# First feed-forward product as seven block products over two row blocks, with row sums shared with the keys, and the second product as a phase of its own fed from DRAM

## The chip, the cores and the metric

The kernel runs on one core of one Trainium2 chip. The metric is the device time of one execution in microseconds; three executions of the kernel before took 507.57, 507.62 and 509.29 us, and the median, 507.62 us, is the number to compare with. TensorE (PE) multiplies matrices, VectorE (DVE), ScalarE (ACT) and GpSimd (POOL) work on tiles of up to 128 partitions, and SyncE (SP) issues nearly all transfers between DRAM and the on-chip memories: SBUF, and PSUM, into which TensorE accumulates.

## The reference

A row x (2048 rows of 512) goes through two branches that a gate mixes:

```python
q, k, v = split(x @ wqkv)                        # 32 heads of 16
phi(t) = [softmax(t @ w_phi), softmax(-t @ w_phi)]
a = (phi(q) @ (phi(k).T @ v)) / (phi(q) @ sum(phi(k)) + 1e-6) @ wo
r = relu(x @ w1 + b1); b = (r * r) @ w2 + b2     # 512 -> 1792 -> 512
g = sigmoid((x * gate_w).sum(-1)); out = g * a + (1 - g) * b
```

All of it is float32. Each operand of a large product is split into two float32r tiles, hi (a copy that ACT makes) and lo (source minus hi, one subtraction), and `mm3` issues three matmuls, hi·hi, hi·lo and lo·hi, into one PSUM tile.

## The kernel before

The rows stand in four blocks of 512 (b), each of four chunks of 128 (c). Blocks of 128 of the 1792 hidden columns are numbered fc (14 of them). The kernel makes two sweeps over the row blocks, sweep 0 with fc 0 to 6 and sweep 1 with fc 7 to 13. In each step of a sweep `up` multiplies one fc of w1 with one row block: four k-slices of 128 by three matmuls of 128x512, so 12 matmuls into one PSUM tile u. `hidden` (L457) turns u into the second product's input: ACT adds the bias and takes relu, squares, and copies hi; DVE subtracts lo (L464). `down` then multiplies that pair with w2 for the four chunks, 12 more matmuls, two steps after (LAG). Sweep 0's results go to a DRAM tile `part` and come back in sweep 1.

Between these steps stand the pieces of the attention branch. In sweep 0 keys and values of two chunks at a time (a pair) come from seven block products of a Strassen-Winograd scheme, p1 to p7, instead of eight: `product` (L549) multiplies row blocks A11, A12, A22 or sums S1 to S4 of them with weight blocks B or differences T1 to T4. The sums of rows are made on POOL (`rows_make`, L276), those of weights on DVE (`sums_make`, L257), before their splits. `features` computes phi(k) on DVE and ACT, `do_kv` accumulates phi(k).T v. In sweep 1 `do_q` and `q_phi` make phi(q) (with two POOL multiplications per chunk, L387), `numer` and `attended` the output of the branch.

The order of all this is written out: `at(slot, f, ...)` puts a piece at a half step of the sweeps, and `tc.issue_after` and `tc.high_priority` bind single instructions; the framework's scheduler orders the rest and sets the waits. Each engine works its own queue strictly in order, so an instruction that waits holds all behind it, on SP too. The weights w1, w2 are split once; lo is kept in DRAM (`lkept`) and hi is copied again from the reloaded source.

Of the kernel before, what the change touches and what calls it, by code (L numbers as in the profile page):

```python
# [23 lines left out]
NFH = NF // 2  # L24
LAG = 2
NG = 8
VW = DH + 1
NV = 2
NPAIR = S // P // 2
NSTR = 3  # L30
AHEAD = 150
FOLD_AT = 9, 3
KEPT_LATE = ("w1", 0), ("w1", 1), ("w2", 0)
SUMS = ("t1", "t2", "t15", "k2")
# [3 lines left out]
def tile_gated_mix(ctx: ExitStack, tc: tile.TileContext, xT, xn, wqT, wkT, wphi, wv, wo, w1, b1, w2, b2, gw, out):  # L38
# [3 lines left out]
    stage = pool("stage", 4)  # L42
    xpool = pool("xpool", 2 * NK)
    wpool = pool("wpool", 1)
    fpool = pool("fpool", NSTR)
# [3 lines left out]
    ps_d = pool("ps_d", NC, space=PSUM)  # L49
    ps_u = pool("ps_u", 2, space=PSUM)  # L50
    ps_a = pool("ps_a", 1, space=PSUM)
    ps_b = pool("ps_b", 1, space=PSUM)
    banks = [ps_a, ps_b]
    st, up_w, down_w = {}, {}, {}
    taken = [0]

    def bank(name):
        p = banks[taken[0] % len(banks)]
        taken[0] += 1
        return p.tile([P, 512], F32, tag="s", name=name)  # L60

    def split(src, hi, lo, ehi, elo):
        if ehi is nc.scalar:
            i = nc.scalar.activation(hi, src, AF.Copy)
        else:
            i = ehi.tensor_copy(hi, src)
        st["low"] = elo.tensor_tensor(lo, src, hi.bitcast(F32), ALU.subtract)  # L70
        return i

    def mm3(o, a, b, sa, sb, first, last, **kw):
        (ah, al), (bh, bl) = a, b
        nc.tensor.matmul(o, ah[:, sa], bh[:, sb], start=first, stop=False, **kw)  # L75
        nc.tensor.matmul(o, ah[:, sa], bl[:, sb], start=False, stop=False, **kw)  # L76
        return nc.tensor.matmul(o, al[:, sa], bh[:, sb], start=False, stop=last, **kw)  # L77

    ALL = slice(0, 512)
    halves = (slice(0, 256), slice(256, 512))  # L80


    def load(src):
        t = stage.tile([P, 512], F32, tag="in", name="in")
        nc.sync.dma_start(t, src)
        return t

    def row():
        return work.tile([P, D], F32, tag="row", name="row", bufs=6)

    def slots(op, kk, name, dtype=F32R):
        return [wpool.tile([P, 512], dtype, tag=f"{op}{kk}{j}", name=f"{name}{j}") for j in "hl"]

    def ffn_tiles(nm, fc):
        if fc >= NFH + NSTR:
            return slots(("B21", "T1", "T4", "T3")[fc - NFH - NSTR], int(nm == "w2"), f"{nm}{fc}")
        return (fpool.tile([P, 512], F32R, tag=nm + "h", name=f"{nm}h{fc}"),
                fpool.tile([P, 512], F32R, tag=nm + "l", name=f"{nm}l{fc}"))

    raw = {}

    def fetch(nm, fc, t=None):
        src = w1[fc] if nm == "w1" else w2[fc * P:(fc + 1) * P, :]
        if t is None:
            t = load(src)
        else:
            nc.sync.dma_start(t, src)
        raw[nm, fc] = t  # L110

    def keep(nm, fc):
        nc.sync.dma_start(lkept[fc, int(nm == "w2")], (up_w if nm == "w1" else down_w)[fc][1].bitcast(F32))

    def again(nm, fc):
        fetch(nm, fc)
        hi, lo = raw[nm, fc, "hl"] = ffn_tiles(nm, fc)
        nc.sync.dma_start(lo.bitcast(F32), lkept[fc, int(nm == "w2")])

    def again_ready(nm, fc):  # L120
        hi, lo = raw.pop((nm, fc, "hl"))
        with tc.issue_after(st["act"].ins):
            nc.scalar.activation(hi, raw.pop((nm, fc)), AF.Copy)
        (up_w if nm == "w1" else down_w)[fc] = hi, lo

    def ready(nm, fc, elo=nc.vector):
        hi, lo = ffn_tiles(nm, fc)
        i = split(raw.pop((nm, fc)), hi, lo, nc.scalar, elo)
        (up_w if nm == "w1" else down_w)[fc] = hi, lo
        return i  # L130

    def ready_later(nm, fc, *elo):
        with tc.issue_after(st["act"].ins):
            ready(nm, fc, *elo)

    def x_tiles(b, k):
        return (xpool.tile([P, SB], F32R, tag="xh", name=f"xh{b}_{k}"),
                xpool.tile([P, SB], F32R, tag="xl", name=f"xl{b}_{k}"))


    def x_save(b):
        for k in range(NK):
            for j in range(2):
                nc.sync.dma_start(xkept[b, k, j], st["x", b][k][j].bitcast(F32))

    def load_x(b):
        xs = []
        for k in range(NK):
            xs.append(x_tiles(b, k))
            for j in range(2):  # L150
                nc.sync.dma_start(xs[k][j].bitcast(F32), xkept[b, k, j])
        return xs


    def x_fetch(b):
        for k in range(NK):
            if k % 2 == 0:
                t = work.tile([P, 2 * D], F32, tag="tb", name="xin", bufs=2)
                st.setdefault(("xr", b), []).append(t)
            raw["x", b, k] = t[:, (k % 2) * D:(k % 2 + 1) * D]  # L160
            nc.sync.dma_start(raw["x", b, k], xT[b, :, k, :])
# [40 lines left out]
    def fold(nm, groups=range(NK)):  # L202
# [19 lines left out]
        if groups[-1] < NK - 1:  # L222
            return
# [648 lines left out]
```

## Time and profile before

| | us |
|---|---|
| median of three executions | 507.62 |
| profiled execution, first to last instruction (span) | 505.0 |
| PE busy | 500.7 |
| DVE busy | 405.2 |
| ACT busy | 253.9 |
| POOL busy | 75.6 |
| DMA, all queues, share of 16 engines | 52% |

The profiled execution's time is its span; the 2.6 us between it and the median lie ahead of the first and behind the last instruction and are taken as the same for both kernels. In the rows of the profile a line begins with the engine or the time, then the code line, the operation, and tile out<-in; "xh", "w1h" are hi tiles, "xl", "w1l" lo tiles. Durations of neighbouring rows on an engine may overlap by some tens of nanoseconds, so the distance of two starts is what one costs.

### The profile page before, as it was taken

The numbers are of one execution on the slowest core, as the hardware profiler recorded it, in microseconds if no ns is written. First come the engines' busy times: TensorE is split into PE (matmuls) and PEld (weight loads), VectorE is DVE, ScalarE is ACT, GpSimd is POOL, SyncE is SP. The second block draws the span as 40 slices with busy tenths as digits, with TensorE's granted clock in tenths as the row PEclk, the third lists the DMA queues.
The fourth block names the chain that finished last, engine by engine and source line by source line (L and its number), as shares of the span: only waits on it lengthen the run. The fifth ranks groups of instructions, "written<-read, shape, count | busy, mean of one in ns | idle before, by whom it ended". The sixth has DMA issues, their size and how long they took to land.

```text
span 505.0 us, 9519 instructions
## 1 busy us (share of the span) xinstructions
PE 500.7 (99%) x3616; PEld 404.0 (80%) x3616; DVE 405.2 (80%) x642; ACT 253.9 (50%) x433; POOL 75.6 (15%) x77
## 2 busy tenths in 40 slices
PE   9999999999999999999999999999999999999997
PEld 4878887788888888888888878787887878788876
DVE  4979996898877868797889898968789677798724
ACT  6598573364743646373765653443425353433530
POOL 5304020302050000000004122202122222202100
PEclk9999999999999999999999999999999999999999
DMA  8998888965657656845669161212153321032102
GB/s 296 331 361 299 232 283 270 321 234 192 212 183 245 236 165 208 279 140 155 187 183 311 51 195 52 91 51 92 39 185 96 86 74 44 8 100 82 43 22 83
DMA packets 52437, 84.79 MB, mean 168 GB/s; under 512 B 8104, under 2 KB 14504, under 8 KB 52392
## 3 DMA queue, kind: packets, MB, share of 16 engines
q1 hardware_dynamic: 52072, 83.79, 51.5%
q8 instruction: 28, 0.46, 0.4%
q10 hardware_dynamic: 288, 0.39, 0.3%
q14 instruction: 17, 0.14, 0.1%
q0 software_dynamic: 32, 0.01, 0.0%
HBM read 56.37 MB, written 21.50 MB: 154 GB/s over the span
## 4 chain that ended last, share of the span: by engine, by line
PE 97%; ACT 1%; DMA 1%; DVE 0%; issue 0%
PE d L75 10%; PE u L75 10%; PE d L77 10%; PE d L76 10%; PE u L76 10%; PE u L77 10%; PE q L75 3%; PE q L77 3%; PE att L77 3%; PE q L76 3%; PE att L76 3%; PE att L75 3%; PE ky L75 2%; PE ky L76 2%; PE ky L77 2%; PE kvps L378 2%
## 5 line engine op out<-in xcount | busy, mean ns | idle before, releaser
L459 ACT ACTIVATE r<-u,b1c 128x512 f32<-128x512 f32 x56 | 38.4, 685 | 146.1 <-PE u L77 146.0
L387 POOL TENSOR_TENSOR ez<-e,z 128x512 f32<-128x512 f32 x32 | 41.3, 1312 | 279.8 <-ACT e L358 160.5
L75 PE MATMUL d<-w2h,hh 128*128 128x512 f32 x160 | 62.7, 392 | 0.0
L77 PE MATMUL d<-w2h,hl 128*128 128x512 f32 x160 | 62.3, 389 | 0.0
L76 PE MATMUL d<-w2l,hh 128*128 128x512 f32 x160 | 62.3, 389 | 0.0
L75 PE MATMUL u<-xh,w1h 128*128 128x512 f32 x152 | 59.6, 392 | 0.1
L76 PE MATMUL u<-xl,w1h 128*128 128x512 f32 x152 | 59.2, 389 | 0.0
L77 PE MATMUL u<-xh,w1l 128*128 128x512 f32 x152 | 59.2, 389 | 0.0
L363 DVE TENSOR_REDUCE sm<-e 128x64 f32<-128x1024 f32 x32 | 38.9, 1215 | 18.5 <-ACT e L358 18.5
L464 DVE TENSOR_TENSOR hl<-r,hh 128x512 fp32r<-128x512 f32 x56 | 38.5, 687 | 13.8 <-ACT hh L463 13.7
L411 ACT ACTIVATE phiT<-tb 32x256 f32<-32x256 f32 x64 | 26.5, 413 | 32.1 <-DVE tb L405 31.4
L358 ACT ACTIVATE e<-e 128x1024 f32<-128x1024 f32 x32 | 33.8, 1056 | 11.9 <-DVE e L356 11.6
L463 ACT ACTIVATE hh<-r 128x512 fp32r<-128x512 f32 x56 | 35.3, 630 | 1.5
L460 ACT ACTIVATE r<-r 128x512 f32<-128x512 f32 x56 | 35.2, 629 | 1.3
L75 PEld LDWEIGHTS d<-w2h,hh 128*128 128x128 f32 x160 | 30.0, 188 | 6.7 <-issue 0.6
L77 PEld LDWEIGHTS d<-w2h,hl 128*128 128x128 f32 x160 | 30.0, 188 | 6.3
L76 PEld LDWEIGHTS d<-w2l,hh 128*128 128x128 f32 x160 | 30.1, 188 | 6.1
L75 PEld LDWEIGHTS u<-xh,w1h 128*128 128x128 f32 x152 | 28.5, 188 | 7.6 <-issue 0.8
L276 POOL TENSOR_TENSOR row<-xin 128x256 f32<-128x256 f32 x16 | 17.5, 1103 | 112.8 <-DVE S2ol L70 24.8
L77 PEld LDWEIGHTS u<-xh,w1l 128*128 128x128 f32 x152 | 28.5, 188 | 6.1
L76 PEld LDWEIGHTS u<-xl,w1h 128*128 128x128 f32 x152 | 28.5, 188 | 5.8
L389 DVE TENSOR_REDUCE dz<-ez 128x64 f32<-128x1024 f32 x16 | 19.4, 1210 | 9.4 <-POOL ez L387 9.3
(544 smaller groups left out, 1161.6 us busy)
## 6 DMA issues: line engine op xcount, KB each, us to landing
in<-in_w SPq DMA_DIRECT2D x66, 256.0 KB, 3.3
phiT<-tb SPq DMA_DIRECT2D x192, 32.0 KB, 1.9
w2l<-lkept SPq DMA_DIRECT2D x20, 256.0 KB, 3.7
w1l<-lkept SPq DMA_DIRECT2D x19, 256.0 KB, 4.4
xin<-in_xT SPq DMA_DIRECT2D x16, 256.0 KB, 5.0
xkept<-xh SPq DMA_DIRECT2D x16, 256.0 KB, 3.6
xkept<-xl SPq DMA_DIRECT2D x16, 256.0 KB, 4.0
in<-in_xn SPq DMA_DIRECT2D x16, 256.0 KB, 2.8
```

Source lines behind the costliest of these rows:

```text
L75: nc.tensor.matmul(o, ah[:, sa], bh[:, sb], start=first, stop=False, **kw)
L76: nc.tensor.matmul(o, ah[:, sa], bl[:, sb], start=False, stop=False, **kw)
L77: return nc.tensor.matmul(o, al[:, sa], bh[:, sb], start=False, stop=last, **kw)
L358: nc.scalar.activation(ef, ef, AF.Exp)
L363: nc.vector.tensor_reduce(sm, e3, AX.X, ALU.add)
L387: nc.gpsimd.tensor_tensor(ez[:, hs, :], e3[:, hs, :], zbc[half], ALU.mult)
L389: nc.vector.tensor_reduce(dz, ez, AX.X, ALU.add)
L411: nc.scalar.activation(dst, src, AF.Copy)
L459: nc.scalar.activation(r, ps, AF.Relu, bias=b1c[:, fc:fc + 1])
L460: nc.scalar.activation(r, r, AF.Square)
L463: st["act"] = nc.scalar.activation(hh, r, AF.Copy)
L464: low = lambda: st.update(low=nc.vector.tensor_tensor(hl, r, hh.bitcast(F32), ALU.subtract))
```

## The change

The first product is put into the same seven-product scheme as the keys and values. The 512 columns of x are halves 1 and 2, the rows of two row blocks are halves 1 and 2, and two fc make one pair g (7 pairs, 2 row pairs r: 14 units u = (r, g)). A unit is seven products of two k-slices by three matmuls, 42 matmuls, where four cells of `up` were 48. Its x operands A11, A12, A22, S1 to S4 are 512 columns wide and are the same tiles that the keys' products read (128 columns of them at a time). Its weight operands per pair are O0 (B11 and B21), O1 (T1 and B22), O2 (T2 and T3) and O3 (T4), made by `w_sums` and `w_last`, mostly on POOL, split, and written to DRAM (`wkept`, `wkept4`) for the second row pair, which reads them back (`w_again`).

The seven results of a unit are combined by adds: t1 is copied by ACT, t15 and t2 are copied by ACT and added to t1 on POOL (`u_half`, L220), three outputs are added on DVE (`u_out`, L211). `hidden` now only does relu and square, in place, and the float32 result goes to a DRAM tile `hkept` (56 tiles of 256 KB). The weight sums of keys and values (`k_ready`) move to POOL.

There are now three phases: an opening (units (0,0) to (0,2), no key products), a phase where the items of `u_stream` and `v_stream` alternate (units of r = 0, then r = 1, with eight key/value pairs of two chunks), and a phase for the second product, queries and output, where `h_fetch` loads each h tile from DRAM, ACT copies hi and POOL subtracts lo (`h_ready`). `part` and the sweeps are gone. TensorE's queue is the order in which the code is written (`manual_schedule`); the other queues are ordered by the framework.

```diff
+    def w_sums(g, eng, tag=None):
+        a, b = raw["w", g, 0], raw["w", g, 1]
+        t = raw["w", g, 2] = ring("T23in") if tag is None else slot(tag, "T23in")
+        eng.tensor_tensor(t[:, RIGHT], b[:, RIGHT], b[:, LEFT], ALU.subtract)
+        eng.tensor_tensor(b[:, LEFT], b[:, LEFT], a[:, LEFT], ALU.subtract)
+        eng.tensor_tensor(t[:, LEFT], b[:, RIGHT], b[:, LEFT], ALU.subtract)
...
+    def uproduct(ps, g, p, first, last):
+        xo, wop = PAIRS[p]
+        t, at = w_op(g, wop)
+        for kk in range(2):
+            mm3(ps, t, st["X", xo, kk], slice(at + kk * P, at + (kk + 1) * P), ALL, first and kk == 0, last and kk == 1,
+                skip_group_check=True)
...
+    def hidden(t, b, f, src):
+        nc.scalar.activation(t, src, AF.Relu, bias=b1c[:, f:f + 1])
+        nc.scalar.activation(t, t, AF.Square)
+        nc.sync.dma_start(hkept[b, f], t)
...
+    def u_half(u, p, key, bankkey):
+        st[bankkey, u] = ubank("u" + bankkey)
+        uproduct(st[bankkey, u], u[1], p, True, False)
+        t = st[key, u] = work.tile([P, 512], F32, tag="ol", name=key, bufs=2)
+        with ahead():
+            nc.scalar.activation(t, st[bankkey, u], AF.Copy)
+            nc.gpsimd.tensor_tensor(t, t, st["t1", u], ALU.add)
...
-    def sums_make(kk, early):
-        k1, k2, v1, v2 = st["w", "k"][kk], st["w", "k"][2 + kk], raw["v", kk], raw["v", 2 + kk]
-        t1, t4 = [raw.setdefault((op, kk), row()) for op in ("T1", "T4")] if early else (raw["T1", kk], raw["T4", kk])
-        raw["T2", kk], raw["T3", kk] = v2, v1
-        for o, x, y in ((t1, v1, k1), (v1, v2, v1)) if early else ((v2, v2, t1), (t4, k2, v2)):
-            nc.vector.tensor_tensor(o, x, y, ALU.subtract)
+    def k_ready(op, kk, eng):
+        k1, k2, v1, v2 = st["w", "k"][kk], st["w", "k"][2 + kk], raw["v", kk], raw["v", 2 + kk]
+        if op == "T1":
+            eng.tensor_tensor(k1, v1, k1, ALU.subtract)
+        elif op == "T3":
+            eng.tensor_tensor(v1, v2, v1, ALU.subtract)
+        elif op == "T2":
+            eng.tensor_tensor(v2, v2, k1, ALU.subtract)
+        elif op == "T4":
+            eng.tensor_tensor(k2, k2, v2, ALU.subtract)
...
+    def h_ready(t):
+        hi, lo = st["h", t] = [work.tile([P, 512], F32R, tag=f"O{t % 2}{j}", name="h" + j, bufs=2) for j in "hl"]
+        split(raw["h", t], hi, lo, nc.gpsimd)
...
+    UP = ("p1", "p5", "p6", "p4", "p2", "p7", "p3")
+    VP = ("p1", "p6", "p5", "p2", "burst", "p7", "p3", "p4")
```

What stands in the queues is shown at three places of the opening. First POOL. Before, these eight rows (sums of two column pieces of x for the first two pairs of chunks, L276) are all of POOL's arithmetic until four more such rows some 25 us later:

```order
L276 TENSOR_TENSOR row_279<-xin_134,xin_135 128x256
L276 TENSOR_TENSOR row_280<-xin_134 128x256
L276 TENSOR_TENSOR row_279<-row_279,xin_134 128x256
L276 TENSOR_TENSOR row_376<-xin_134,xin_135 128x256
L276 TENSOR_TENSOR row_280<-xin_135,row_279 128x256
L276 TENSOR_TENSOR row_376<-row_376,xin_134 128x256
L276 TENSOR_TENSOR row_377<-xin_134 128x256
L276 TENSOR_TENSOR row_377<-xin_135,row_376 128x256
```

Now the queue holds six 128x512 sums of x (S1, S2, S4), nine 128x256 sums of w1 and four t15/t2 adds, and behind these the twelve rows below, up to T2 (L283) of both k-slices:

```order
L152 TENSOR_TENSOR T23in_621<-w1in_508 128x256
L153 TENSOR_TENSOR w1in_508<-w1in_508,w1in_506 128x256
L154 TENSOR_TENSOR T23in_621<-w1in_508 128x256
L279 TENSOR_TENSOR wkin_464<-wvin_155,wkin_464 128x512
L220 TENSOR_TENSOR t15_535<-t15_535,t1_242 128x512
L281 TENSOR_TENSOR wvin_155<-wvin_156,wvin_155 128x512
L283 TENSOR_TENSOR wvin_156<-wvin_156,wkin_464 128x512
L158 TENSOR_TENSOR w1in_506<-w1in_506,T23in_621 128x256
L220 TENSOR_TENSOR t2_583<-t2_583,t1_242 128x512
L279 TENSOR_TENSOR wkin_464<-wvin_155,wkin_464 128x512
L281 TENSOR_TENSOR wvin_155<-wvin_156,wvin_155 128x512
L283 TENSOR_TENSOR wvin_156<-wvin_156,wkin_464 128x512
```

That is 31 rows (18 of 128x512, 13 of 128x256) where there were eight of 128x256. Second DVE, at the split of the same operand T2. Before, DVE makes the differences itself (L257) and splits right behind them (L70):

```order
L257 TENSOR_TENSOR wvin_224<-wvin_224,row_426 128x512
L257 TENSOR_TENSOR wvin_224<-wvin_224,row_430 128x512
L257 TENSOR_TENSOR row_427<-wkin_353,wvin_224 128x512
L257 TENSOR_TENSOR row_431<-wkin_353,wvin_224 128x512
L70 TENSOR_TENSOR T20l_499<-wvin_224,T20h_498 128x512
L70 TENSOR_TENSOR B210l_503<-wkin_353,B210h_502 128x512
L70 TENSOR_TENSOR T21l_507<-wvin_224,T21h_506 128x512
```

Now the splits (L57) wait for POOL's differences, mixed with the unit outputs c (L211), and T2's second slice is the 52nd row of DVE's queue:

```order
L57 TENSOR_TENSOR O0l_607<-w1in_506,O0h_606 128x512
L57 TENSOR_TENSOR KB111l_515<-wkin_464,KB111h_514 128x512
L57 TENSOR_TENSOR O1l_669<-w1in_508,O1h_668 128x512
L57 TENSOR_TENSOR KT10l_520<-wkin_464,KT10h_519 128x512
L211 TENSOR_TENSOR c_616<-uY_576,t15_535 128x512
L57 TENSOR_TENSOR KT11l_525<-wkin_464,KT11h_524 128x512
L57 TENSOR_TENSOR KT31l_565<-wvin_155,KT31h_564 128x512
L211 TENSOR_TENSOR c_631<-uZ_528,t2_583 128x512
L57 TENSOR_TENSOR KT20l_588<-wvin_156,KT20h_587 128x512
L57 TENSOR_TENSOR KT21l_593<-wvin_156,KT21h_592 128x512
```

Third PE, where the first product with T2 stands (p6 of the first key pair, tile ky before, kY now). Before, it stands inside a cell of the first product (u), after two of its matmuls:

```order
L75 MATMUL u_609<-xh0_0_164,w1h6_534 128x512
L76 MATMUL u_609<-xl0_0_165,w1h6_534 128x512
L75 MATMUL ky_644<-T20h_498,S0oh0_368 128x512
L76 MATMUL ky_644<-T20l_499,S0oh0_368 128x512
L77 MATMUL ky_644<-T20h_498,S0ol0_370 128x512
```

Now it is the 22nd whole product, counted from unit (0,1)'s p1, with p5 of unit (0,3) ahead of it and that unit's p6 (tile uY_722, operand O2) behind:

```order
L61 MATMUL uZ_701<-S11h_231,O1h_668 128x512
L62 MATMUL uZ_701<-S11l_232,O1h_668 128x512
L63 MATMUL uZ_701<-S11h_231,O1l_669 128x512
L61 MATMUL kY_713<-KT20h_587,S20h_264 128x512
L62 MATMUL kY_713<-KT20l_588,S20h_264 128x512
L63 MATMUL kY_713<-KT20h_587,S20l_265 128x512
L61 MATMUL kY_713<-KT21h_592,S21h_268 128x512
L62 MATMUL kY_713<-KT21l_593,S21h_268 128x512
L63 MATMUL kY_713<-KT21h_592,S21l_269 128x512
L61 MATMUL uY_722<-S20h_264,O2h_681 128x512
```

Products of six matmuls have taken the place of cells of twelve, and TensorE's queue can't pass T2's product before both slices of T2 are split.

1174 lines of the change are left out of this document (618 added, 556 removed).

## The prediction

> **What bounds the kernel now.** I read the page first: busy times, the slices, and the chain that ended last.
>
> ```profile
> span 505.0 us, 9519 instructions
> ...
> PE 500.7 (99%) x3616; PEld 404.0 (80%) x3616; DVE 405.2 (80%) x642; ACT 253.9 (50%) x433; POOL 75.6 (15%) x77
> ...
> DVE  4979996898877868797889898968789677798724
> ...
> POOL 5304020302050000000004122202122222202100
> PEclk9999999999999999999999999999999999999999
> ...
> PE 97%; ACT 1%; DMA 1%; DVE 0%; issue 0%
> ```
>
> TensorE is busy all the time at its full granted clock and is 97% of the chain. Busy alone could hide small waits, so next the view of waits for PE, the chain's first and last pieces, and four neighbouring matmuls of the timeline:
>
> ```profile
> PE warm L500 <- PEq L861: 0.8, 1, 0.8
> PE u L527 <- DMA win<-in_w: 0.3, 1, 0.3
> ```
>
> ```profile
> 5.42 3.70 PE u L527 x8
> ...
> 17.34 1.84 PE foldk L211 x102
> ...
> 501.89 0.48 DVE row L817
> ```
>
> ```profile
> 182.81 0.39 PE L75 MATMUL u<-xh,w1h 128*128 128x512 f32 x1
> 183.04 0.39 PE L76 MATMUL u<-xl,w1h 128*128 128x512 f32 x1
> 183.26 0.39 PE L77 MATMUL u<-xh,w1l 128*128 128x512 f32 x1
> 183.49 0.39 PE L75 MATMUL u<-xh,w1h 128*128 128x512 f32 x1
> ```
>
> Three matmuls start within 183.49 - 182.81 = 0.68 us, so one costs 0.2267 us, not its 0.39. From 5.42 to 501.89 the profile names no wait for PE of over a microsecond. **The kernel is bound by the number of matmuls**: every one saved is worth 0.2267 us as long as its operands keep coming in time, and every wait that appears is added in full.
>
> **The change, part by part.**
>
> *Matmuls.* Before, the first product is 14 x 4 cells of 12; now it is 14 units of 42. One whole cell of float32 matmuls at the start (L527) stays, in place of a unit's p1 and p2 and worth 12 in both. So 672 - 588 = 84 matmuls go. Keys, queries, output and the second product keep theirs. 84 x 0.2267 = **-19.0 us**. That is all the change can win.
>
> *The opening.* Here POOL gets work that it didn't have, and DVE's splits run beside it. What they do to each other shows in the timeline of both engines, in three stretches:
>
> ```profile
> 12.55 1.22 DVE L70 TENSOR_TENSOR w2l<-win,w2h 128x512 fp32r<-128x512 f32 x1
> 14.11 0.81 DVE L464 TENSOR_TENSOR hl<-r,hh 128x512 fp32r<-128x512 f32 x1 [0.34 <-ACT hh L463]
> 14.85 1.22 DVE L70 TENSOR_TENSOR w1l<-in,w1h 128x512 fp32r<-128x512 f32 x1
> ...
> 37.71 0.69 DVE L464 TENSOR_TENSOR hl<-r,hh 128x512 fp32r<-128x512 f32 x1
> 38.31 0.69 DVE L70 TENSOR_TENSOR w1l<-in,w1h 128x512 fp32r<-128x512 f32 x1
> ...
> 43.72 0.68 DVE L354 TENSOR_REDUCE mn<-kx 128x32 f32<-128x512 f32 x1
> 44.32 0.68 DVE L355 TENSOR_TENSOR e<-kx,mx 128x512 f32<-128x512 f32 x1
> ```
>
> ```profile
> 13.19 1.19 POOL L276 TENSOR_TENSOR row<-row,xin 128x256 f32<-128x256 f32 x1
> 14.34 1.18 POOL L276 TENSOR_TENSOR row<-xin 128x256 f32<-128x256 f32 x1
> ...
> 43.88 0.74 POOL L276 TENSOR_TENSOR row<-row,xin 128x256 f32<-128x256 f32 x1
> 44.58 0.75 POOL L276 TENSOR_TENSOR row<-xin 128x256 f32<-128x256 f32 x1
> ...
> 270.21 2.54 POOL L387 TENSOR_TENSOR ez<-e,z 128x512 f32<-128x512 f32 x2 [2.42 <-DVE dz L389]
> ```
>
> Alone, a DVE split costs 38.31 - 37.71 = 0.60 us, a POOL sum of 256 columns 44.58 - 43.88 = 0.70, one of 512 columns 2.54 / 2 = 1.27. At 12 to 16 us both engines work on two SBUF tiles at once, and there a split lasts 1.22 and a POOL sum 1.18: POOL starts one each 14.34 - 13.19 = 1.15 us, about a sum and a split one after the other. At 44 us DVE reads PSUM, and neither is slowed. So two-SBUF-tile operations of DVE and POOL take turns. A pair of a 256-column sum and a split costs 1.15 us; with a 512-column sum 1.27 - 0.70 = 0.57 more, 1.72.
>
> The Trainium skill, page "SBUF — State Buffer", section "Who interferes with whom", says the same against this change: a DVE instruction with two SBUF inputs and a GpSimd instruction that reads SBUF exclude each other for the whole instruction. By it the opening is the turn-taking sum below, 45.9 us and not POOL's 32.0 alone. The rows at 12 to 16 us agree.
>
> Up to T2's last split the change's queues hold 31 POOL sums (18 of 512 columns, 13 of 256), and from the first of them on 35 DVE rows with two SBUF tiles (30 of 512). Pairing them: 13 x 1.15 + 18 x 1.72 = 45.9 us. Start:
>
> ```profile
> 7.90 1.88 POOL L276 TENSOR_TENSOR row<-xin 128x256 f32<-128x256 f32 x2 [4.81 <-DMA xin<-in_xT]
> ```
>
> ```profile
> GB/s 0 0 38 197 246 303 398 379 358 355 402 396 393 402 391 393 385 377 339 396 391 396 393 369 290 145 243 363 350 328 257 268 347 385 284 216 238 371 377 322
> ```
>
> Before, POOL starts at 7.90, when the four tiles of the first row block have landed. S1 needs tiles of the second row block, up to the ninth of the opening's 256 KB loads. The view of the DMA over the first 30 us (0.75 us a slice) reaches 9 x 0.262 MB at 9.2 us; I take 9.5. Then T2 is split at 9.5 + 45.9 = 55.4 us if somebody always works. Not so: three times POOL has nothing to do until TensorE has made a product (t15 of unit (0,1), its t2, and the weights' transposes after the fold), each a round through PE, ACT and DVE, while DVE does some eight rows alone. I estimate 7 us left idle by both, from products of 6 x 0.2267 = 1.36 us and two or three rows of 0.6 behind each. **T2 at 62.4 us.**
>
> TensorE, if nothing held it up, would be there at 5.42 + 3.70 + 21 products x 1.36 + 1.84 for the fold = 39.5 us. So it waits 22.9 us in the opening. A further wait follows: p6 of unit (0,3) needs O2's split, which stands in DVE's queue behind t2 of the key product that was just released (1.36 us) and four and a half splits (3.4 us with t2), of which TensorE fills 1.36. That is 3.4 us. Opening: **+26.3 us**. Bounds: if POOL and DVE did not hinder each other, POOL's own queue would end at 9.5 + 18 x 1.27 + 13 x 0.70 = 41.5, a wait of 2.0 and the 3.4 behind it, +5; if the idle rounds cost double, +34.
>
> *The middle phase.* A key/value pair and a unit now take 84 matmuls and the phi(k) burst:
>
> ```profile
> 105.36:130.13 24.77, 24.77 (x237) 20.39 (x240) 22.40 (x40) 13.92 (x25) 3.17 (x4) 1.00 0.65 216
> 130.13:154.81 24.68, 24.68 (x239) 20.34 (x241) 19.73 (x30) 13.21 (x21) 6.58 (x8) 1.00 0.64 214
> ```
>
> ```profile
> 130.13 1.31 PE kvps L378 x100
> ```
>
> ```profile
> L363 DVE TENSOR_REDUCE sm<-e 128x64 f32<-128x1024 f32 x32 | 38.9, 1215 | 18.5 <-ACT e L358 18.5
> L369 DVE TENSOR_TENSOR e<-e,r 128x1024 f32<-128x1024 f32 x16 | 19.4, 1214 | 0.0
> L365 DVE RECIPROCAL r<-sm 128x64 f32<-128x64 f32 x32 | 17.3, 541 | 0.0
> L568 DVE TENSOR_TENSOR t<-ky,t 128x512 f32<-128x512 f32 x8 | 5.5, 683 | 0.0
> L324 DVE SCALAR_TENSOR_TENSOR in<-in,gwb 128x512 f32<-128x512 f32 x16 | 11.4, 712 | 3.1 <-DMA w1l<-lkept 3.1
> ```
>
> Before, a key/value pair went by in 24.7 us, with DVE busy for (22.40 + 19.73) / 2 = 21.1. Now it has 84 x 0.2267 + 1.31 = 20.4 us. DVE's share is two features (four rows like 0.68, then 1.21, 0.54, 1.21: 5.7 each), five adds and three unit outputs of 0.68, kvs (0.4) and 3.5 splits of 0.69: 19.6 us of durations in 27 rows; neighbours overlap by 0.69 - 0.60 = 0.09, so 17.2. POOL adds per pair 2 x 1.27 + 4 x 0.70 = 5.3 us, and about a third of DVE's rows read two SBUF tiles: 1.7 us of turns. 18.9 of 20.4 fits with little to spare. It doesn't fit where the row pair changes: 14 splits of x and 11 gate rows of 0.71 come on top, and POOL has the sums of x again; there DVE has some 29 us of work for 26 us of products. I take **+4 us**, bounds 0 and 12.
>
> *The last phase.* It has the old matmuls, DVE without the 56 lo splits of h, and on POOL 56 of them at 1.27 where a step of the second product alone lasts 12 x 0.2267 = 2.7 us. The four h tiles give two steps of lead over a load. **+1 us**, bounds 0 and 4. The transfers that come in for the old ones (56 h tiles out and in, seven w tiles a unit) I cost at nothing:
>
> ```profile
> q1 hardware_dynamic: 52072, 83.79, 51.5%
> ```
>
> Half of the DMA engines' time is free, and h and w are asked for a step or more ahead; if that cover went, each late w tile would cost TensorE part of a landing.
>
> **Sum**: 505.0 - 19.0 + 26.3 + 4 + 1 = 517.3 us of span, and 507.62 - 505.0 = 2.6 around it, as before: **519.9 us**. The forecast's own range is 508 to 528: below, the rounds lose nothing and O2 is in time (55.4 - 39.5 = 15.9 in place of 26.3); above, the opening's upper bound.
>
> **Rivals.**
>
> *POOL and DVE work side by side* (faster). If the opening's DVE rows fall into gaps that POOL leaves anyway, the opening costs 5 instead of 26: 519.9 - 21 = 498.6; with a middle phase without loss 494.6. For it: at 44 us POOL's sums take 0.74 beside DVE. Against it: there DVE reads PSUM, while nearly all of the opening's rows are splits. It decides if POOL's 31 sums average less than 1.1 us.
>
> *Matmuls alone* (faster): the splits and sums are ahead everywhere, 505.0 - 19.0 + 2.6 = 488.6. For it: PE's waits before are 1.1 us in all. Against it: POOL's own queue ends behind TensorE's need even undisturbed (41.5 against 39.5).
>
> *The clock falls* (slower still). In the opening TensorE would wait several microseconds at a time, which it never did before. If the granted clock halves after such waits, products cost twice 1.36 us; with 6 of the 21 products on the rounds that POOL waits for, +8 us, 528. For and against there is only PEclk at 9 in every slice, under a load without waits. The Trainium skill, page "TensorE: Matmul & The Clock Gate", section "HAM oscillation — how this bites in real kernels", says that idle gaps beyond about 3.4 us drop the clock; no run here has such a gap.
>
> **How the numbers follow.** Forecast 0.60; side by side 0.18; matmuls alone 0.07; clock 0.15. Half a per cent (2.5 us, about what a measurement of this kernel can tell from no change) puts "same" at 505.1 to 510.2. Faster: 0.18 + 0.07 = 0.25. Same: the forecast's lower edge, 0.06. Slower: 0.69. The range leaves out matmuls alone and the upper half of the clock case: 494 to 530.
>
> **What would show it.** Right: PE's slices below 9 between 20 and 75 us and full behind; T2's first product (kY) near 62 us; POOL sums of 512 columns at 1.7 us and more there, DVE splits at 1.2; pitch still 0.2267. The middle would show as waits of kvps or of products with O2 on DVE rows around the change of row pair. Wrong: kY before 50 us, or PEclk below 9. The forecast falls if DVE's rows stand before POOL's in time, so that each finds the other idle; and it is too low if SP's queue, where weight loads now stand behind stores that wait for ACT, brings the third pair's weights late.

## The result, and the profile after

| | before | changed |
|---|---|---|
| median of 4 runs, us | 507.6 (507.2 to 509.29) | 566.85 (563.45 to 567.68) |
| ratio, 95% interval | | 1.1154 (1.1116 to 1.1191) |
| profiled execution, span and time, us | 505.0, 507.6 | 565.7, 567.48 |
| matmul instructions | 3616 | 3532 |
| mean granted clock in the span | 1.00 | 0.957 |

The change makes the kernel 11.5% slower. The forecast was 519.9 us in a range of 494 to 530: right in the direction, 47 us too low in size. The page of the changed kernel shows busy times, the slices and the chain that ended last:

```profile
span 565.7 us, 9750 instructions
...
PE 504.6 (89%) x3532; PEld 396.0 (70%) x3532; DVE 432.4 (76%) x621; ACT 259.8 (46%) x447; POOL 216.7 (38%) x176
...
DVE  4977759989999998667959999763578676687503
...
POOL 3946734174252022123144463351335252434420
PEclk9889869999999999999999979999699997999999
...
PE 46%; DVE 30%; DMA 8%; issue 6%; ACT 6%; POOL 3%; SPq 1%; DVEq 0%; POOLq 0%; ACTq 0%
```

TensorE was 97% of the chain before and is 46% now. PEclk has digits below 9 in seven slices, four of them among the first six and three far behind: the loss has several places. The view of waits for PE (engine and line, what it waited for, total us, times, longest) names them:

```profile
PE att L63 <- DVE ol L57: 11.0, 4, 5.2
PE uX L61 <- ACT t L205: 6.7, 2, 5.0
PE d L61 <- ACT w210h L56: 4.8, 1, 4.8
PE d L62 <- DVE w210l L57: 4.7, 1, 4.7
PE uY L61 <- ACT O2h L56: 3.7, 2, 3.5
...
PE kY L61 <- ACT KT20h L56: 3.3, 1, 3.3
```

uX, uY and kY are the opening; d and att are the last phase, where the prediction had put one microsecond. The view by stretches (span of the stretch; busy time of PE, PEld, DVE, ACT and POOL; then the granted clock) has both:

```profile
20.00:40.00 20.00, 13.80 (x44) 10.03 (x44) 18.30 (x19) 13.18 (x25) 14.57 (x13) 0.83 0.42 155
60.00:80.00 20.00, 10.71 (x27) 6.99 (x26) 11.05 (x15) 10.66 (x20) 11.14 (x10) 0.66 0.73 261
305.00:320.00 15.00, 12.56 (x56) 10.07 (x54) 15.00 (x20) 4.82 (x9) 7.19 (x5) 1.00 0.25 67
320.00:335.00 15.00, 7.96 (x23) 6.00 (x24) 15.00 (x20) 9.65 (x17) 8.87 (x6) 0.66 0.57 195
395.00:410.00 15.00, 8.82 (x25) 6.72 (x26) 8.76 (x13) 5.88 (x13) 6.53 (x6) 0.66 0.23 66
```

Before, PE was busy for 19.86 and 20.00 of 20 us and for 15.00 of 15 us in these stretches. The distance of two starts of 128x512 matmuls, less the full pitch of 0.2267 us, is what TensorE lost between them. Added up over the trace, this gives the account of the 60.7 us by which the span grew, plus the 19.0 that the fewer matmuls saved, 79.7 in all:

- up to 80 us: 25.2 us in eleven waits of 0.9 us and more, and 6.2 us in 31 matmuls that started about 0.43 us apart instead of 0.2267
- from 80 us to the first d (276 us): 7.6 us in six waits
- from the first d to the end: 25.3 us in seven waits over 0.67 us, 11.0 us in shorter ones and slow matmuls

That is 75.3; of the rest, 1.8 us is a wait at 7.6 us inside the first float32 cell, the other 2.6 lie in short waits and smaller matmuls.

### The profile page after: what moved, and what is told of

It is laid out like the page before. It is cut to its first block, busy times and chain, and to the rows that moved or that the text cites. A ratio compares the mean times of both kernels' runs of the same rounds, so it can differ in the third digit from the quotient of the medians.

```text
span 565.7 us, 9750 instructions
## 1 busy us (share of the span) xinstructions
PE 504.6 (89%) x3532; PEld 396.0 (70%) x3532; DVE 432.4 (76%) x621; ACT 259.8 (46%) x447; POOL 216.7 (38%) x176
## 4 chain that ended last, share of the span: by engine, by line
PE 46%; DVE 30%; DMA 8%; issue 6%; ACT 6%; POOL 3%; SPq 1%; DVEq 0%; POOLq 0%; ACTq 0%
PE d L61 6%; PE d L62 6%; PE d L63 6%; DMA w1in<-in_w 3%; PE att L63 3%; DVE xnin L406 2%; DVE e L307 2%; PE att L61 2%; PE att L62 2%; DVE e L320 2%; DVE mx L304 2%; PE uY L63 2%; PE q L61 2%; DVE sm L314 2%; DVE mn L305 2%
## 5 line engine op out<-in xcount | busy, mean ns | idle before, releaser
L57 POOL TENSOR_TENSOR hl<-hin,hh 128x512 fp32r<-128x512 f32 x56 | 73.3, 1318 | 143.0 <-ACT hh L56 135.2
L220 POOL TENSOR_TENSOR t<-t,t 128x512 f32<-128x512 f32 x28 | 42.1, 1506 | 100.8 <-ACT t L219 87.7
L56 ACT ACTIVATE hh<-hin 128x512 fp32r<-128x512 f32 x56 | 34.5, 624 | 48.2 <-issue 19.7
L309 ACT ACTIVATE e<-e 128x1024 f32<-128x1024 f32 x32 | 33.8, 1056 | 40.6 <-DVE e L307 40.4
L196 ACT ACTIVATE c<-c,b1c 128x512 f32<-128x512 f32 x42 | 30.0, 718 | 38.2 <-DVE c L211 38.1
L197 ACT ACTIVATE c<-c 128x512 f32<-128x512 f32 x56 | 34.9, 627 | 1.1
L211 DVE TENSOR_TENSOR c<-uY,t 128x512 f32<-128x512 f32 x28 | 18.9, 676 | 5.4 <-PE uY L63 5.4
L320 DVE TENSOR_TENSOR e<-e,r 128x1024 f32<-128x1024 f32 x16 | 21.5, 1346 | 0.2
L510 DVE STREAM_TRANSPOSE tb<-e 128x1024 f32<-128x1024 f32 x16 | 19.8, 1235 | 0.4
L57 DVE TENSOR_TENSOR ol<-num,oh 128x512 fp32r<-128x512 f32 x16 | 10.4, 684 | 12.6 <-ACT oh L56 12.6
L320 DVE TENSOR_TENSOR e<-e,w 128x1024 f32<-128x1024 f32 x16 | 19.6, 1224 | 0.3
L316 DVE RECIPROCAL r<-sm 128x64 f32<-128x64 f32 x32 | 17.4, 543 | 0.2
```

Source lines behind the costliest of these rows:

```text
L196: nc.scalar.activation(t, src, AF.Relu, bias=b1c[:, f:f + 1])
L197: nc.scalar.activation(t, t, AF.Square)
L220: nc.gpsimd.tensor_tensor(t, t, st["t1", u], ALU.add)
L309: nc.scalar.activation(ef, ef, AF.Exp)
L320: eng.tensor_tensor(e3, e3, w.unsqueeze(2).to_broadcast([P, 2 * H, DH]), ALU.mult)
```

## The experiments

Each kernel ran beside the kernel before, whose median was 507.2 to 507.8 us every time. Three figures of the trace tell the places apart: when the first product with T2 starts (kY), when the first matmul of the second product starts (d), and how long it is from there to the last matmul. All are edits of the changed kernel. In e12 and e17 the hi tile takes the place of the lo tiles that are left out: as many matmuls are timed, but the result loses the precision of the split.

| kernel | what | time, us | kY | first d | from d to end |
|---|---|---|---|---|---|
| changed | | 566.9 | 64.5 | 276.0 | 286.0 |
| e1 | opening's sums on DVE | 553.8 | 64.0 | 266.0 | 283.5 |
| e8 | e1 in another order | 556.0 | 56.1 | 265.6 | 283.9 |
| e2 | output stores on POOL's queue | 572.3 | 63.9 | 275.9 | 290.0 |
| e3 | h's lo splits on DVE | 565.5 | 64.1 | 277.6 | 280.5 |
| e4 | x loads on POOL's queue | 566.0 | 64.5 | 276.6 | 284.4 |
| e5 | six row buffers | 567.3 | 64.6 | 277.1 | 284.0 |
| e6 | e3, h's loads on POOL's queue | 557.5 | 64.9 | 276.3 | 276.3 |
| e7 | added products in six waits | 562.1 | 66.9 (behind the added products, from 64.1 on) | 278.0 | 279.4 |
| e9 | rows filled by DVE, not ACT | 557.3 | 64.2 | 277.8 | 274.4 |
| e10 | query chunks later | 564.6 | 64.3 | 277.2 | 281.7 |
| e11 | e8 + e6 + e9 + e10 | 542.6 | 56.1 | 266.0 | 270.5 |
| e12 | 32 lo splits left out | 561.7 | 62.0 | 273.1 | 284.2 |
| e13 | e11, added products in waits | 536.5 | 55.9 | 261.8 | 267.6 |
| e14 | e3, phi's transfers on POOL's queue | 565.8 | 64.9 | 276.4 | 280.8 |
| e15 | e13 with e14's queue for e6's, no added products behind d | 537.1 | 55.5 | 261.7 | 269.7 |
| e16 | e15 without e10 | 544.3 | 56.9 | 262.2 | 274.7 |
| e17 | e14 without w2's and wo's lo splits | 558.7 | 63.8 | 277.2 | 274.0 |
| e18 | e13, buffers and lead of h's loads | 537.3 | 57.2 | 262.2 | 270.4 |

**The opening: turns of DVE and POOL (e1, e8).** The two engines' timelines in the changed kernel, POOL's sums first (an add of a unit's halves takes as long), DVE's splits behind:

```profile
52.70 1.72 POOL L220 TENSOR_TENSOR t<-t,t 128x512 f32<-128x512 f32 x1
54.38 1.74 POOL L281 TENSOR_TENSOR wvin<-wvin 128x512 f32<-128x512 f32 x1
```

```profile
20.84 1.21 DVE L57 TENSOR_TENSOR O1l<-w1in,O1h 128x512 fp32r<-128x512 f32 x1
21.98 1.21 DVE L57 TENSOR_TENSOR S11l<-S1in,S11h 128x512 fp32r<-128x512 f32 x1
```

Here a 512-column sum takes 1.72 us where it took 1.27 alone, and a split 1.21 where it took 0.60, as predicted; over the first 70 us the 35 splits of 512 columns take 1.06 us on average. e1 takes the sums off POOL:

```diff
-            x_sums(kk, ("S1",), POOLE)
+            x_sums(kk, ("S1",), DVEE)
...
-                k_ready(op, kk, POOLE)
+                k_ready(op, kk, DVEE)
```

> All sums of the opening (x, w1 and key operands) go from POOL to DVE; only the units' t15 and t2 adds stay on POOL. Turn-taking theory: a 512-column sum and a split cost 1.72 us as a pair of POOL and DVE, 1.2 us as two DVE rows; DVE's splits fall from 1.2 to 0.6-0.7 us there, the first kY product starts near 55 us in place of 64.3, and the time falls by 8 to 12 us, to about 556. Rival, POOL's rows are long by themselves or the rounds between the engines set the opening: DVE has 15 us more in its queue and nothing is won back, kY at 64 us or later, 567 to 580.

Measured 553.8, 13 us less: DVE does some 15 us of sums more and the phase is still shorter, with splits of 0.73 us on average over the first 70 us. So the turns are real. But kY stood at 64.0 instead of the 55 expected: unit (0,3)'s split O1l came behind a dozen key rows and TensorE waited 8.9 us for it at 53 us. e8 puts O1, B22 and T2 ahead of B21, T3 and T4:

```diff
-        for op in ("T3", "B22"):
-            for kk in range(2):
-                k_ready(op, kk, POOLE)
+        for kk in range(2):
+            k_ready("B22", kk, DVEE)
...
+        w_ready(3, 1)
         w_save(2, 1)
...
-        for kk in range(2):
-            k_ready("T4", kk, POOLE)
-        w_ready(3, 1)
+        for op in ("B21", "T3", "T4"):
+            for kk in range(2):
+                k_ready(op, kk, DVEE)
```

> As e1 (all sums of the opening on DVE), and the splits of unit (0,3)'s second weight tile and of B22 and T2 stand ahead of those of B21, T3 and T4. Theory that the opening is now DVE's own queue in its order: the stall of 8.9 us at 53 us (O1l behind ten key rows) falls to 2 to 4 us, time 546 to 550. Rival, TensorE is held by the sum of DVE's rows whatever their order: the stall comes back at T3 or T4, 553 us.

kY now starts at 56.1, and nothing is won by it: first d 265.6 against e1's 266.0, 556.0 us. Three rows of e8's TensorE, in order of start, and the next wait:

```profile
59.12 0.50 PE L61 MATMUL uY<-S20h,O2h 128*128 128x512 f32 x1 [1.44 <-ACT O2h L56]
59.45 0.40 PE L62 MATMUL uY<-S20l,O2h 128*128 128x512 f32 x1
62.80 0.79 PE L63 MATMUL uY<-S20h,O2l 128*128 128x512 f32 x1 [2.94 <-DVE O2l L57]
```

The stall has moved to O2: the rival's reading. So taking the turns away, at the price of more rows on DVE, wins about 10 us. That the number of DVE's rows holds the rest, whatever their order, is argued from this one move; no run took rows out of e8's opening.

**The last phase, single edits (e2 to e5, e9, e10).** The longest wait of the view is att's for ol. ACT and SP ahead of it, in the changed kernel:

```profile
375.98 0.63 ACT L56 ACTIVATE hh<-hin 128x512 fp32r<-128x512 f32 x1 [2.22 <-issue]
389.22 0.72 ACT L557 ACTIVATE row<-b2b,rest 128x512 f32<-128x512 f32 x1 [12.61 <-DMA out<-row]
392.75 0.72 ACT L557 ACTIVATE row<-b2b,rest 128x512 f32<-128x512 f32 x1 [2.81 <-DMA out<-row]
...
395.37 1.06 ACT L56 ACTIVATE oh<-num 128x512 fp32r<-128x512 f32 x2
```

```profile
369.06 16.24 SPq L518 DMA_DIRECT2D phiT<-tb  x24
385.40 0.52 SPq L69 DMA_DIRECT2D hin<-hkept  x1
386.02 0.38 SPq L564 DMA_DIRECT2D out<-row  x1
```

ACT fills an output row with the bias and stands 12.6 us until an older row has been stored; the store is issued behind 24 transfers of phi; oh, for which TensorE waits, stands behind the fill. So does ACT's e (L309), for which DVE stands idle 8.5 us; DVE's ol, the longer part of the stall, comes seven rows later in its queue, at 401.2. Three edits at this chain: the stores on another queue, one more row buffer, and no fill at all.

```diff
-            nc.sync.dma_start(out[n * P:(n + 1) * P, :], st["f", n])
+            nc.gpsimd.dma_start(out[n * P:(n + 1) * P, :], st["f", n])
```

> The stores of finished output rows are issued by POOL's queue in place of SP's. Theory of the row buffers: the five row buffers come free late because their stores stand in SP's queue behind 24 transfers of phi that wait for DVE; ACT's waits for a free row (47.3 us at L557) fall below 10, the stalls of att at 393, 396, 461 and 462 us (13.7 us together) go, and some of the slow clock behind them: about 549 us. Rival, DVE bounds the last phase (it is busy in 49.9 of 50 us at 300 to 350): the stalls come back as waits on DVE's rows, 560 us or more.

```diff
-    row = lambda name="row": work.tile([P, 512], F32, tag="row", name=name, bufs=5)
+    row = lambda name="row": work.tile([P, 512], F32, tag="row", name=name, bufs=6)
```

> One more row buffer (6, as in the kernel before; the room comes from the gate weights, which now lie in a buffer of x). Theory of the row buffers: ACT's waits for a free row (47.3 us at L557) fall to under 15, the stalls of att at 393, 396 and 462 us (13 us) go with a part of the slow clock behind them: 549 to 553 us. Rival, as in the run with the stores on another queue: what ends the wait is the end of the attended product itself, and the stalls only move: 560 us or more.

```diff
-            nc.scalar.activation(st["f", n], st["b2b"], AF.Copy, scale=rest[:, n:n + 1])
...
-            nc.vector.tensor_tensor(t, ps, t, ALU.add)
+            nc.vector.scalar_tensor_tensor(t, st["b2b"] if new else t, rest[:, n:n + 1], ps, ALU.mult, ALU.add)
```

> ACT no longer fills output rows ahead: the first of attend and evict to touch a row takes the bias in with its own DVE instruction, so no DVE row is added and 16 ACT rows go. Theory: ACT's queue holds these fills long before their step and stands there (47.3 us at L557) until an old row has been stored, with oh of the waiting att behind it; the stalls of att at 393, 396 and 462 us (13 us) go, with 3 to 5 us of slow clock: 548 to 553 us. Rival, DVE's ol is late by itself: the stalls stay as waits for ol, 560 us or more.

e2 gave 572.3 and e5 567.3: both missed, with 30.4 and 40.0 us of ACT's row waits left. The row that ACT fills at 389 us belongs to a later step; a buffer more, or an earlier store, is used up by a fill still further ahead (that reading of e5 is argued, not measured). e9 gave 557.3, 9.6 us less, and of the long att stalls only one stayed (5.1 us at 452 us); from 380 to 410 us PE is busy all 30.0 us. So the fills held up about 10 us.

At 317 to 322 us the waits are for w210 (4.8 and 4.7 us in the view of waits). SP, ACT and DVE ahead of it, in the changed kernel:

```profile
307.46 8.13 SPq L518 DMA_DIRECT2D phiT<-tb  x12
315.69 0.53 SPq L69 DMA_DIRECT2D xin<-in_xT  x1
```

```profile
320.35 0.63 ACT L56 ACTIVATE xS11h<-xin 128x512 fp32r<-128x512 f32 x1 [4.40 <-DMA xin<-in_xT]
...
321.64 0.63 ACT L56 ACTIVATE w210h<-w2in 128x512 fp32r<-128x512 f32 x1
```

```profile
325.97 1.70 DVE L57 TENSOR_TENSOR w210l<-w2in,w210h 128x512 fp32r<-128x512 f32 x1
```

SP stood 5.1 us until DVE had the first tb ready, then issued 12 small transfers of phi for 8.1 us, and only then a tile of x; ACT waited for that tile with w210h behind it. The second wait is DVE's: w210's lo split starts 3.7 us after w210h was ready. e3 gave DVE h's lo splits back, e4 took the x loads out of SP's queue, e10 began the query chunks later:

```diff
-        split(raw["h", t], hi, lo, nc.gpsimd)
+        split(raw["h", t], hi, lo)
```

> The 56 lo splits of h go from POOL back to DVE. Theory that POOL's splits stretch DVE's rows in the last phase by turns: DVE's busy time there does not grow although it has 34 us of rows more, and the time falls by about 10 us, to 557. Rival, the last phase is held up by SP's queue and ACT's order, DVE's stretching is hidden: DVE has 34 us more work, the stalls at 317 to 322 and 393 to 396 us stay, and the time is 567 to 585.

```diff
-            src = load(ring("xin"), xT[b, :, kk, :])
+            src = ring("xin")
+            nc.gpsimd.dma_start(src, xT[b, :, kk, :])
```

> The loads of x for the last phase (x_again, 2 raw tiles and the kept ones) are issued by POOL's queue in place of SP's. Theory of SP's queue: the split of xS11 on ACT no longer waits 4.4 us for xin, w210h behind it is in time, and the stalls of d at 317 and 322 us (10.1 us) go with some slow clock behind them: about 553 us; the row waits at 393 and 461 stay. Rival, the stall there comes from ACT waiting for DVE's e, or POOL now waits for a free buffer ahead of its h splits: 563 us or more.

```diff
-        starts = (2, 7, 12, 18, 24, 30, 36, 42)
+        starts = (2, 9, 15, 20, 25, 30, 36, 42)
```

> The query chunks of the last phase start later (steps 2, 9, 15, 20, 25, 30, 36, 42 in place of 2, 7, 12, 18, 24, 30, 36, 42), nothing else. Theory that DVE is overloaded in the first 14 steps, where the splits of w2 and wo stand beside the features (49.9 of 50 us busy at 300 to 350): the stalls of d at 317 and 322 us (10.1 us) shrink to under 4, time 556 to 561. Rival, the stall is made by SP's queue (xin behind phi) and stays: 565 us or more.

565.5, 566.0 and 564.6 against the changed kernel's runs of 563.45 to 567.68: no difference that these runs can tell; all three expectations were missed. In e3 the stall at 317 came back as 3.3 + 5.2 + 2.2 us at 311 to 332, in e10 as one of 9.0 at 320.

**Two causes at one place (e6, e12, e14, e17).** e6 takes h's loads out of SP's queue:

```diff
-        raw["h", t] = load(ring("hin"), hkept[ORDER_B[i], f])
+        raw["h", t] = ring("hin")
+        nc.gpsimd.dma_start(raw["h", t], hkept[ORDER_B[i], f])
```

> The lo splits of h on DVE as in e3, and the loads of h issued by POOL's queue instead of SP's. Theory of SP's queue: loads of h stand behind 12 transfers of phi that wait for DVE (one h load was issued at 318.2 us in e3, right behind twelve that began at 310.5); taken out of that queue, the stalls of d at 311 to 332 us (10.7 us) go with some slow clock, 4 to 8 us from the stores and row waits stay: about 553 us. Rival, DVE is the bound there (15.0 of 15 us busy at 305 to 320): the stall stays as a wait for splits on DVE, 562 us or more.

557.5, 8 us less than e3, 4.2 of them between the first d and the end; but the stall of d stayed, 5.4 + 5.2 + 2.3 us at 310 to 334, and what shrank were the later ones. e12 takes DVE rows away instead, with h's splits still on POOL (keys and wo in the same manner):

```diff
-        split(raw["w2", f], *t)
-        st["w2", f] = t
+        nc.scalar.activation(t, raw["w2", f], AF.Copy)
+        st["w2", f] = t, t
```

> The lo splits of the key operands (14), of w2 (14) and of wo (4) are left out; the products use the hi tile in their place, so TensorE has as many matmuls and DVE 32 rows less. Theory that DVE's queue bounds both places: in the opening kY starts 6 to 8 us earlier (56 to 58 us in place of 64.5); in the last phase the stalls of d at 317 and 322 us (10.1 us) go with the slow clock behind them, and the phase from the first d to the end falls from 286 to 272 us, though the row waits at 393 to 462 us stay: 545 to 552 us in all. Rival, loads in SP's queue and ACT's order hold these places: kY over 62 us, the last phase over 282, 560 us or more.

561.7 us; kY 62.0 and the last phase 284.2: the rival. One stall of 8.0 us at 311, and SP's queue and ACT show why:

```profile
299.50 7.19 SPq L518 DMA_DIRECT2D phiT<-tb  x11
306.73 0.58 SPq L458 DMA_DIRECT2D woin<-in_wo  x1
307.42 7.47 SPq L518 DMA_DIRECT2D phiT<-tb  x12
314.99 0.53 SPq L69 DMA_DIRECT2D hin<-hkept  x1
```

```profile
317.91 0.63 ACT L56 ACTIVATE hh<-hin 128x512 fp32r<-128x512 f32 x1 [6.88 <-DMA hin<-hkept]
318.49 0.63 ACT L474 ACTIVATE w29h<-w2in 128x512 fp32r<-128x512 f32 x1
```

From 299.5 on SP issues phi's small transfers for 15.4 us, one load of wo among them, 14.66 / 23 = 0.64 us each; it is issuing all that while. The load of h stands behind them and is issued at 315.0, and w29, which TensorE waits for, stands behind hh on ACT. e14 then moves phi's transfers, with DVE's rows all there:

```diff
-                    nc.sync.dma_start(dst, src)
+                    nc.gpsimd.dma_start(dst, src)
```

> As e3 (h's lo splits on DVE), and the 192 small transfers that turn phi are issued by POOL's queue instead of SP's; loads and stores stay on SP. Theory that phi's transfers hold SP's queue (in e12 23 of them and one load took it from 299.5 to 315.0 us, and the h and w2 loads behind them came 8 us late): the stalls of d at 311 to 332 us in e3 (10.7 us) and most of those of att at 399, 462 and 521 us (8.3 us) go with their slow clock, 545 to 550 us. Rival, DVE's and ACT's own order: the stalls stay, 560 us or more; or POOL's ez rows now come late behind the transfers, over 566 us.

565.8 us: the rival again. The stall stands at 310 to 331 us (3.4 + 6.0 + 3.0), now with DVE at its end. TensorE's and DVE's rows of e14:

```profile
320.59 0.39 PE L62 MATMUL d<-w29l,hh 128*128 128x512 f32 x1
326.81 0.79 PE L63 MATMUL d<-w29h,hl 128*128 128x512 f32 x1 [5.83 <-DVE hl L57]
```

```profile
315.89 2.28 DVE L504 TENSOR_TENSOR w<-r,den 128x64 f32<-128x64 f32 x1
...
326.08 0.68 DVE L57 TENSOR_TENSOR hl<-hin,hh 128x512 fp32r<-128x512 f32 x1
```

hh was ready at 317.4 (it started at 316.73), its lo split came 8.7 us later in DVE's queue. Each edit had found the other cause waiting. e17 does both:

> e14 (phi's transfers on POOL's queue, h's lo splits on DVE) and, as in e12, the lo splits of w2 and wo left out (the hi tile stands in their place; the keys keep theirs). Theory of two causes, each enough by itself: h's next load waits for SP's queue and for a buffer that DVE's splits give back, so e12 and e14, which took one each, kept the stall; with both taken the stalls of d at 310 to 332 us (12.4 us in e14) fall under 4, the time from the first d to the last matmul from 281 (e14) and 284 (e12) to 266 to 272, 550 to 555 us in all. Rival, a third thing (ACT's order, the rounds of the query features) holds these steps: 278 or more, 560 us and up.

Between 280 and 345 us no wait of TensorE over 1 us is left. The view by stretches of e17, beside the changed kernel's 12.56 and 7.96 us of PE:

```profile
305.00:320.00 15.00, 14.81 (x66) 11.94 (x65) 14.41 (x24) 13.40 (x26) 12.67 (x26) 1.00 0.72 226
320.00:335.00 15.00, 14.26 (x89) 10.91 (x88) 13.11 (x24) 6.83 (x13) 8.30 (x13) 1.00 0.59 193
```

So at this place two causes stand in parallel, each enough by itself: loads (of h, x and w2) behind phi's transfers in SP's queue, and splits of h, w2 and wo among the features in DVE's. The size was missed all the same (558.7 for 550 to 555): a new stall of 7.9 us in two waits stands at 346 to 357 us, where the row block changes. Ahead of the longer one ACT waited 2.6 us for h's load, and h's lo split came 4.8 us after hh, behind rows of the query features on DVE.

**The clock (e7, e13).** After many waits TensorE's matmuls start about 0.43 us apart for some microseconds. e11's rows around a wait of 2.3 us at the change of row pair:

```profile
155.05 0.40 PE L61 MATMUL uY<-S31h,O2h 128*128 128x512 f32 x1
157.59 0.80 PE L62 MATMUL uY<-S31l,O2h 128*128 128x512 f32 x1 [2.14 <-DVE S31l L57]
158.18 0.63 PE L63 MATMUL uY<-S31h,O2l 128*128 128x512 f32 x1
158.61 0.63 PE L61 MATMUL kZ<-KT10h,S10h 128*128 128x512 f32 x1
```

158.61 - 158.18 = 0.43 us, and so on up to 163.7: 14 matmuls, 3.0 us above the full pitch. The view by stretches shows the granted clock there (the third figure from the end), with PE busy nearly all the time:

```profile
157.50:163.50 6.00, 5.91 (x14) 4.67 (x15) 3.81 (x7) 1.35 (x2) 0.00 (x0) 0.50 0.66 220
```

It reads 0.50; from 150 to 156 and from 164.5 to 170 us it reads 1.00. To tell the clock from late operands by an edit too, products that add zero were put into the waits:

```diff
+    def filler(o, n, start=False):
+        one = nc.const_aps.tensor(1.0, (P, P), mybir.dt.bfloat16)
+        for _ in range(n):
+            nc.tensor.matmul(o, one, zeros, start=start, stop=False, skip_group_check=True)
```

> Small bf16 products that add zero are put ahead of the waiting matmuls at six places where the changed kernel's TensorE stands still 2.5 to 5.4 us (kY's first product, p6 of unit (0,3), w210's two matmuls, att of two pairs); nothing else differs. Theory of the clock: the granted clock no longer falls after these waits, the slow matmuls (21 us above the full pitch in all, most of them behind these six) go: 550 to 558 us. Rival, the clock falls for another reason, or the matmuls behind the waits are slow because their operands come late: 564 to 572 us.

> e11 with bf16 products that add zero ahead of the matmuls that wait there 1.6 to 4.4 us (six places). Theory of the clock: in e11 five of these waits are each followed by 4 to 6 us of matmuls at half pitch, 11.8 us above the full pitch together; with the engine kept busy through them the time falls by 8 to 12 us, to 531 to 535. Rival, the pitch behind a wait is slow because operands come one by one: 541 to 545 us.

e7: 562.1, between the two expectations, with the mean granted clock at 0.979 for 0.957. In the last phase 3 matmuls are left at the slow pitch, for 31; the stretches at 0.50 that remain, at 19, 53 and 169 us, stand behind waits without added products. e13: 536.5 (ratio to before 1.0577, 1.0557 to 1.0598) against e11's 542.6, 6 us of the 8 to 12 expected. PEclk by slices, e11 and then e13:

```profile
PEclk9979799999989999999999799899999999999999
```

```profile
PEclk9999999999999999999999998999999999999999
```

With the engine kept busy the slow pitch is gone but for one stretch, behind a wait of 3.3 us at 320 us that had no added products (9 matmuls, 1.8 us lost): it is the clock, not the operands.

**All together (e11, e15, e16, e18).**

These have no edits of their own but e18:

```diff
-            src = load(ring("xin"), xT[b, :, kk, :])
+            src = load(row("xin"), xT[b, :, kk, :])
...
-                h_fetch(t + 2)
+                h_fetch(t + 3)
```

> Together: the opening of e8, the h loads and splits of e6, the rows of e9, the starts of e10. If the causes add up: 566.9 - 11 (opening) - 9 (h queue) - 14 (rows) - 6 (starts) = 527 us; with the stalls of the opening and of the first steps partly back, up to 540. In no case under 507: the opening and the change of row pair still cost over 25 us together.

> As e13, but phi's transfers on POOL's queue and the h loads back on SP's, without the two places of added products in the last phase. SP-queue theory: the last phase, 271 us from the first d to the end in e11 and 268 in e13, falls to 255 to 260, near its matmuls' 252; 522 to 527 us in all. Rival, moving the h loads had already taken out all that SP's queue costs: 533 to 538 us.

> As e15 with the query chunks' starts back at 2, 7, 12, 18. If DVE's load in the first 14 steps counts: 4 to 8 us above e15. If SP's queue alone held these steps: equal to e15 within 2 us.

> e13 with the raw x tiles of the last phase in a row buffer instead of two of the four buffers that h's loads use, and h asked for three steps ahead instead of two. Theory that h's load waits for a buffer: e13's stall at 293 us (3.2 us) goes, the one at 320 shrinks, 268 us from the first d to the end become 262 to 265, 531 to 534 us in all. Rival, DVE's order alone: 535 us or more.

e11 gave 542.6, above its range: in the last phase the parts don't add up (9.7 + 11.6 + 4.3 us alone, 15.5 together). e15 tells no difference between moving h's loads and moving phi's transfers (537.1 and 536.5, though e15 also lacks the added products of the last phase); its theory, 522 to 527, was missed. e16, 7 us above e15, shows that DVE's load in the first steps does count once SP's queue is clear, though e10 alone had won next to nothing. e18 missed too: other buffers for x and a step more lead for h's loads won nothing, so e13's last stalls aren't a matter of buffers. The best version, e13, is 30 us better than the changed kernel and 5.8% slower than before. None beats before.

## Why the prediction was wrong

*Matmuls, -19.0.* Right: 84 fewer, and the pitch is 0.2267 wherever the clock is full.

*The opening, +26.3.* The size of the waits came out (25.2 us in eleven, and 1.8 in the float32 cell), and so did T2's time, kY at 64.5 for 62.4, but in part by luck. The turns are there: the 31 sums average 1.32 us, above the 1.1 by which the rival of engines side by side was to be judged. Yet the sums took 40.8 us, not 45.9 (18 of 512 columns at 1.54 on average, 13 of 256 at 1.00), and POOL stood idle for 13.5 us in five gaps, not 7 in three; the two errors nearly cancel. O2's wait at 68.6 us was 4.0 + 1.1 for 3.4. TensorE's two rows:

```profile
60.77 0.39 PE L63 MATMUL uZ<-S11h,O1l 128*128 128x512 f32 x1
64.49 0.49 PE L61 MATMUL kY<-KT20h,S20h 128*128 128x512 f32 x1 [3.33 <-ACT KT20h L56]
```

Too much was put on the turns, though: undone in e8, with more rows on DVE in exchange, they give back 10 us of the 25. And the first waits come earlier than any of POOL's rounds, at 12 and 17 us, where ACT's t stood behind splits of w1: at 12 us one that waited for its load, at 17 us two that waited for DVE's sums.

*The clock.* It was a rival at 0.15 and +8 us, and it came: 6.2 us of slow matmuls in the opening, 12.4 in the whole (62 matmuls). It should have been a term of the sum, since the forecast itself had waits of several microseconds.

*The middle phase, +4 (0 to 12).* In its bounds: 7.6 us, most of it at 151 to 168 us where the row pair changes, the longest (2.3 us) for S31's split; DVE was busy in 29.98 of the 30 us from 160 on.

*The last phase, +1 (0 to 4).* **This is the step that failed**, by 35 of the 47 us. It was argued that "the four h tiles give two steps of lead over a load", and the new transfers were costed "at nothing" because "half of the DMA engines' time is free". Neither says when a load is issued. The loads stand in SP's in-order queue behind phi's transfers: in the changed kernel 5.1 us until the first could go and 8.1 us for issuing 12 of them, in e12 15.4 us for issuing alone. These transfers are not new: before, 24 of them took SP's queue 15.1 us (from 299.9 us on), but the next things behind those were two output stores. And the cover on DVE that the step counted on (56 splits moved to POOL) was not there in the first 14 steps, since w2's and wo's splits stand there too: 15.0 of 15 us busy. Each is enough alone (e12, e14); with both gone the place is free (e17). The third part, ACT filling rows ahead and standing on it, 10 us (e9), was in no step at all. The text's last sentence named SP's queue, but for the weights of the third pair.

*Outside the span, 2.6.* 567.48 - 565.7 = 1.8.

Open stays what of e13's 10 us of waits and slow matmuls in the last phase is DVE and what ACT's order, and whether an opening with fewer DVE rows could reach its matmuls.

## What to carry to other kernels

Free bandwidth says nothing of a load that stands in an in-order queue behind others: for every transfer that a change adds, name what is ahead of it in its queue, how long that takes to issue and what it waits for. Count an engine's load per stage, not per phase: DVE had room over the last phase as a whole and none in its first 14 steps. When an edit that should help changes nothing, look for a second cause at the same place and take both away before the theory is dropped; and cost every wait of TensorE of some 2 us and more with the slow matmuls behind it.

## What the runs showed of the hardware

The granted clock can fall after shorter waits than expected. Where the row pair changes, the changed kernel and fourteen of the edits (all but e13, e15, e16 and e18, which have added products there) have the same two waits, of 1.2 to 1.3 and of 2.3 us, with four matmuls between them. In the changed kernel full pitch follows. In the fourteen others 6 to 13 matmuls at 0.427 us follow: right behind the wait in nine of them, after three to five matmuls at full pitch in e4, e5, e6, e10 and e14. So length alone doesn't decide. In the profiles' record of the granted clock every stretch at 0.50 that ends within the span lasts 3.41 us or two, three or four times that (e11 from 156.9 to 163.7 us), and the pitch in it is 0.427 us. The Trainium skill, page "TensorE: Matmul & The Clock Gate", section "HAM oscillation — how this bites in real kernels", puts the point at gaps beyond about 3.4 us; the waits of 3.5 us and more here agree, all 62 of them in the changed kernel and the edits were followed by a stretch at 0.50; the one of 2.3 us lies below it, and the clock fell all the same.

Issuing has a price of its own. SyncE starts one of phi's 192 transfers (32 KB) each 0.63 us, before as after the change, and GpSimd in e14 one each 0.49 us; a load of h (256 KB) takes SyncE 0.38 us.

A DVE row that reads two SBUF tiles can be held up for much longer than the 0.6 us by which a split grows beside POOL: in e14 w, 0.2 us alone (L397 of before: 0.22), took 2.28 us while POOL's two ez rows ran.
